# A second, narrower arm of the first product for jobs with at most 64 rows

## The chip, the cores and the metric

The kernel runs on one core of one Trainium2 chip. The metric is the device time of one execution in microseconds; several executions are timed and the median is taken.

## The reference

The kernel computes a recurrent attention and hands its output, token by token, to a mixture of experts in which every token goes to one expert. Cut to what matters here:

```python
B, H, S, D = 4, 8, 768, 48
x = attention(r, k, v, w, u)                # (B*S, H*D): 3072 tokens x 384
logits = x @ w_gate + modality_bias[modality_id]        # 8 experts
e_idx = argmax(logits)
gate_w = softmax(logits)[e_idx]
for e in range(8):
    mask = e_idx == e
    h = maximum(x[mask] @ w1[e], 0)         # 384 -> 1024
    out[mask] = gate_w[mask] * (h @ w2[e])  # 1024 -> 384
```

With the drawn inputs three of the eight experts get tokens: 1569, 1354 and 149.

## The kernel before, in words

The first part of the kernel works through the attention in 24 units of 128 tokens. As tokens are finished they are written as rows to a place of their expert, sorted by expert. While the later units run, nine fixed "slots" already compute 9 x 128 rows of the most popular expert. Of its 1569 rows 417 are left for later.

What is left is done in jobs. A job is up to 128 rows of one expert: 4 jobs for the 417 rows (the last holds 33), 11 for the 1354 (the last holds 74) and 2 for the 149 (the last holds 21), in this order, 17 in all. A job that has fewer rows still computes 128; what stands in the other rows is written nowhere. The first job (key "a") stands ahead of the loop; `tc.For_i` (L1434) runs the other 16, one in each turn, with the same instructions. Its bound `nj` comes from the device.

Which rows and which expert a job has is told by a table that `jobs` (L764 and following) works out on VectorE while the last slots run. It has one column per job (40 at most) and three rows: the first row's number (ROW), a code that says what has to be done for a change of expert (CODE), and the expert to load next (MORE). The table is computed with one job per partition, in `field`. L863 spreads it (product with the identity, `jd`), one matmul of TensorE (L866, `ptab`) brings it onto one partition, and VectorE casts it to integers (`tab`, L868). `at` (L873) reads one entry into a register of the engines that need it: SyncE reads ROW and MORE, ScalarE and VectorE read CODE.

Every number of the matmuls' inputs is split into a high and a low 16-bit half. A job's first product (`up`, `raise_`, L997) multiplies the transposed rows `mxT` by the first weights: `whi` against the high and the low rows, `wlo` against the high rows, three pieces of depth 128 each, so nine terms for each of eight blocks of 128 hidden values: 72 pairs of a weight load and a matmul with 128 columns, one column per row of the job. It goes in three groups of 4, 2 and 2 blocks, each into one tile `phb`. ScalarE takes the high half of the relu out of it (L1001, `hh`), VectorE the low half (L1006, `hl`). The second product (`term`, L1067) has 24 terms of 384 columns: eight of `whi` and eight of `wlo` with `hh` (`high_terms`), and eight of `whi` with `hl` (`low_terms`).

The turn of the loop is staggered by one: it begins with the low terms of the job before, whose output is then scaled, given to GpSimd and written (`put`). Then come the first product of the turn's own job, the load of the next weights (`next_load`, when the table asks), the copy of the following job's rows into place (`take_in`, L1402), and the high terms. The rows of the next job are fetched ahead by SyncE at the turn's start (`turn`). Where the expert changes (turns 4 and 15), ScalarE and VectorE split the new weights: `first_half` at the end of the turn before, `change` with 3, 4 and 5 in the turn itself. These stand under `tc.If`, which ScalarE and VectorE test with the code (L1413, L1424); TensorE tests nothing in a turn but the loop's own end. The order in each engine's queue is that in which the code is written (`manual_schedule`).

Of the kernel before, what the change touches and what calls it, by code (L numbers as in the profile page):

```python
# [12 lines left out]
I32 = mybir.dt.int32  # L13
I16 = mybir.dt.int16
AF = mybir.ActivationFunctionType
ALU = mybir.AluOpType
AX = mybir.AxisListType

P = 128
# [6 lines left out]
E = 8  # L26
# [13 lines left out]
NJ = 40  # L40
# [14 lines left out]
MS = ('DVE', 'Activation', 'PE', 'SP', 'Pool')  # L55
ROW, CODE, MORE = range(3)
SP, ACT, AD = (mybir.EngineType.SP,), (mybir.EngineType.Activation,), (mybir.EngineType.Activation, mybir.EngineType.DVE)
WQ = 2 * WC // NQ
# [6 lines left out]
class _Kernel:  # L65
# [213 lines left out]
    def setup3(self):  # L279

        c, v = self.c, self.nc.gpsimd
        gi, li = c.tile([P, STEPS], I32, name="gridi"), c.tile([P, 1], I32, name="linei")
        self.grid, self.linep, self.least = c.tile([P, STEPS], F32, name="grid"), c.tile([P, 1], F32, name="linep"), c.tile([P, E], F32, name="least")
        self.bits, self.line1 = c.tile([P, STEPS], F32, name="bits"), c.tile([P, 1], F32, name="line1")
        zeros = lambda name, shape: c.tile(shape, F32, name=name)
        self.jb, self.cum, self.ol = zeros("jb", [P, E + 2]), zeros("cum", [P, E + 1]), zeros("ol", [P, 5, E + 1])
        v.iota(gi, pattern=[[-1, STEPS]], base=STEPS - GONE, channel_multiplier=1)
        for q in range(STEPS):
            v.memset(self.bits[:, q : q + 1], float(1 << q))
        v.tensor_scalar_add(self.line1, self.line, -1.0)  # L290
        v.iota(li, pattern=[[0, 1]], base=0, channel_multiplier=P)
        for t in (self.jb, self.cum, self.ol, self.least):
            v.memset(t, 0.0)
        self.two = zeros("two", [P, 2, E])
        self.nc.scalar.copy(self.two[:, 0], self.idx)
        v.memset(self.least[:, :2], 1.0)
        v.tensor_copy(self.grid, gi)
        v.tensor_copy(self.linep, li)
# [473 lines left out]
    def jobs(self):  # L772


        nc, c = self.nc, self.c
        v = nc.vector
        new = lambda name, shape=[P, E], dt=F32: c.tile(shape, dt, name=name)
# [47 lines left out]
        v.scalar_tensor_tensor(ol[:, 2, 1:], act[:, 1:], float(-GONE), cum[:, 1:], ALU.mult, ALU.add)  # L825
        v.tensor_copy(ol[:, 3, 1:], cs)
        yield
        od, jr = new("od", [P, 5, E]), new("jr", [P, 5])
        v.tensor_sub(od, ol[:, :, 1:], ol[:, :, :E])
        yield  # L830
        v.scalar_tensor_tensor(od, cs.unsqueeze(1).to_broadcast([P, 5, E]), self.line, od, ALU.is_le, ALU.mult)
        yield
        v.reduce_sum(jr, od, axis=AX.X)
        yield
        field, past = new("field", [P, 3]), new("past", [P, 1])
        v.tensor_scalar(past, jr[:, 1:2], self.line, float(E * CAP), ALU.is_le, ALU.mult)
# [18 lines left out]
        v.reduce_sum(b, due, axis=AX.X)  # L855
        v.tensor_mul(field[:, MORE : MORE + 1], jr[:, 4:5], now)
        yield
        v.scalar_tensor_tensor(field[:, CODE : CODE + 1], now, float(1 << STEPS), b, ALU.mult, ALU.add)
        yield

        wide = [NJ, 3, NJ]
        d = new("jd", [P, 3, NJ])
        v.tensor_mul(d[:NJ], field[:NJ].unsqueeze(2).to_broadcast(wide), self.id32[:NJ, :NJ].unsqueeze(1).to_broadcast(wide))  # L863
        yield "pe"
        pt = self.ps_s.tile([P, 512], F32, tag="s", name="ptab")
        nc.tensor.matmul(pt[:1, : 3 * NJ], self.ones[:NJ, 0:1], d[:NJ].rearrange("p k j -> p (k j)"), start=True, stop=True)  # L866
        self.tab = new("tab", [1, 3, NJ], I32)
        v.tensor_copy(self.tab.rearrange("p k j -> p (k j)"), pt[:1, : 3 * NJ])  # L868
        yield
# [119 lines left out]

    def raise_(self, ph, f0, fb, t=0):  # L990

        hi, lo = self.whi, self.wlo
        terms = [(hi, dc, xq) for dc in range(DC) for xq in (dc, DC + dc)] + [(lo, dc, dc) for dc in range(DC)]
        for i, (w, dc, xq) in enumerate(terms):
            for q in range(fb):
                c0 = (f0 + q) * DM + dc * P
                self.nc.tensor.matmul(ph[:, q * P : (q + 1) * P], w[:, c0 : c0 + P], self.xT[:, xq, t * P : (t + 1) * P], start=i == q == 0, stop=i == len(terms) - 1, skip_group_check=True)  # L997

# [8 lines left out]

    def up(self, key, beside=lambda: None, late=False):
        later = []
        sizes = [4, 2, 2]  # L1010
        for g, fb in enumerate(sizes):
            f0 = sum(sizes[:g])
            ph = self.ps_a.tile([P, 512], F32, tag="big", name=f"ph{key}{g}")
            self.raise_(ph, f0, fb)
            self.relu_high(ph, f0, fb)
# [74 lines left out]
    def run(self):  # L1090
# [343 lines left out]
        with tc.For_i(1, nj, 1, iteration_sync="reg_based") as i, tc.manual_schedule(engines={getattr(mybir.EngineType, e) for e in MS[:4]}):  # L1434
            self.turn(0, self.at(ROW, i, E * CAP, SP, 1), mn, xn)
            code = self.at(CODE, i, 2 << STEPS, AD)
            self.low_terms(po)
            square(code)
# [4 lines left out]
            beside = iter([lambda: change(code, 5), lambda: self.scales("2")])  # L1443
            self.up("b", lambda: next(beside, lambda: None)(), True)
            next_load()
# [48 lines left out]
```

## Time and profile before

| | us |
|---|---|
| median of 3 runs | 353.31 |
| lowest, highest | 352.26, 354.82 |
| profiled execution, its own time | 353.3 |
| span of the profiled execution | 351.5 |
| TensorE busy in the span | 330.6 |

The span goes from the first to the last instruction; the execution's own time has 1.8 us more around it. PE is TensorE's matmuls, PEld its weight loads, PEldq its sequencer (registers, branches, semaphore steps), DVE VectorE, ACT ScalarE, POOL GpSimd, SP SyncE. Durations overlap: a matmul is shown from its start to its last result (219 ns at 128 columns), and the next starts before that.

### The profile page before, as it was taken

The numbers are of one execution on the slowest core, as the hardware profiler recorded it, in microseconds if no ns is written. First come the engines' busy times: TensorE is split into PE (matmuls) and PEld (weight loads), VectorE is DVE, ScalarE is ACT, GpSimd is POOL, SyncE is SP. The second block draws the span as 40 slices with busy tenths as digits, with TensorE's granted clock in tenths as the row PEclk, the third lists the DMA queues.
The fourth block names the chain that finished last, engine by engine and source line by source line (L and its number), as shares of the span: only waits on it lengthen the run. The fifth ranks groups of instructions, "written<-read, shape, count | busy, mean of one in ns | idle before, by whom it ended". The sixth has DMA issues, their size and how long they took to land. (4 is left out here: it accounts for less than half of the span.)

```text
span 351.5 us, 15420 instructions
## 1 busy us (share of the span) xinstructions
PE 330.6 (94%) x5555; PEld 269.6 (77%) x5555; DVE 220.0 (63%) x740; ACT 179.5 (51%) x476; POOL 154.6 (44%) x230
## 2 busy tenths in 40 slices
PE   7999998969899997999999999998999999999993
PEld 3888898868768885978888777776778888777771
DVE  6878898799898956498458843348423332334850
ACT  7678776867957644667542222247222224553820
POOL 8888678776646762435265711112111120121221
PEclk9999999878999998999999999999999999999999
DMA  6767677999539998736334632116722111112110
GB/s 194 214 157 166 141 174 214 319 263 211 138 112 195 265 208 235 173 103 122 92 92 137 229 118 64 45 45 207 224 53 59 45 45 45 45 45 67 35 45 5
DMA packets 56798, 46.96 MB, mean 134 GB/s; under 512 B 42920, under 2 KB 50359, under 8 KB 56496
## 3 DMA queue, kind: packets, MB, share of 16 engines
q1 hardware_dynamic: 53552, 36.86, 44.2%
q0 software_dynamic: 3200, 9.47, 7.7%
q8 instruction: 31, 0.51, 0.7%
q14 instruction: 15, 0.12, 0.1%
HBM read 26.03 MB, written 11.83 MB: 108 GB/s over the span
## 5 line engine op out<-in xcount | busy, mean ns | idle before, releaser
L997 PEld LDWEIGHTS <-whi 128*128 128x128 f16 x1248 | 72.4, 98 | 3.6 <-issue 0.9
L1067 PEld LDWEIGHTS <-hh 128*128 128x128 f16 x416 | 38.7, 98 | 29.5 <-ACT hh L1001 3.1
L997 PE MATMUL phb<-mxT,whi 128*128 128x128 f16 x768 | 50.7, 219 | 0.0
L410 ACT ACTIVATE dv<-kv,d 128x48 f32<-128x48 f32 x172 | 43.1, 324 | 2.3 <-POOL gap L664 1.8
L1001 ACT ACTIVATE hh<-phb 128x256 f16<-128x256 f32 (+1 forms) x48 | 21.4, 453 | 32.6 <-PE L997 16.9
L997 PEld LDWEIGHTS <-wlo 128*128 128x128 f16 x624 | 37.7, 98 | 0.0
L371 POOL TENSOR_TENSOR rk<-rc,kc 112x512 f32<-112x512 f32 x20 | 25.7, 1286 | 25.0 <-DVE ebx L309 12.0
L430 DVE TENSOR_TENSOR at<-psc,mask 128x512 f32<-128x512 f32 x48 | 31.7, 682 | 6.0 <-PE psc L424 6.0
L1006 DVE SCALAR_TENSOR_TENSOR hl<-phb,hh 128x256 f16<-128x256 f32 (+1 forms) x48 | 24.1, 511 | 17.5 <-ACTq L1424 15.0
L1087 DVE TENSOR_SCALAR fac<-mt,wf 128x1 f32<-128x1 f32 x17 | 3.6, 213 | 49.1 <-ACTq L1424 36.1
L359 POOL TENSOR_TENSOR rc<-ud,powr 112x512 f32<-112x512 f32 (+1 forms) x25 | 31.1, 1248 | 3.6 <-DMA ud<-in_pd 2.6
L966 POOL TENSOR_TENSOR seenb<-otb,putb 128x1 int32<-128x1 int32 x16 | 3.0, 188 | 65.1 <-ACTq L1424 53.2
L1067 PEld LDWEIGHTS <-hl 128*128 128x128 f16 x208 | 19.8, 99 | 14.7 <-issue 2.4
L424 PE MATMUL psc<-rc,kc 64*64 64x128 f32 (+1 forms) x768 | 29.7, 294 | 1.4 <-POOL rc L359 0.7
L957 ACT ACTIVATE otb<-po,fac 128x384 f32<-128x384 f32 x16 | 9.2, 578 | 41.8 <-PE phb L997 41.8
L665 POOL DMA_INDIRECT rows<-row,posi x24 | 24.9, 1039 | 10.4 <-DVE pr L742 3.3
L1067 PE MATMUL po<-whi,hh 128*128 128x384 f16 x136 | 28.3, 327 | 1.1 <-ACT hh L1001 1.0
L997 PE MATMUL phb<-mxT,wlo 128*128 128x128 f16 x384 | 29.3, 219 | 0.0
L1067 PE MATMUL po<-wlo,hh 128*128 128x384 f16 x136 | 28.0, 326 | 1.3 <-DVE wlo L943 1.3
L424 PEld LDWEIGHTS psc<-rc,kc 64*64 64x64 f32 (+1 forms) x768 | 22.9, 143 | 7.9 <-issue 2.7
L943 DVE SCALAR_TENSOR_TENSOR wlo<-raw,ws,whi 128x1024 f16<-128x1024 f32 (+1 forms) x20 | 27.0, 1389 | 1.2 <-ACT whi L938 1.2
L997 PE MATMUL phs<-mxT,whi 128*128 128x128 f16 x432 | 27.2, 219 | 0.0
(272 smaller groups left out, 663.4 us busy)
## 6 DMA issues: line engine op xcount, KB each, us to landing
kv<-in_pt SPq DMA_DIRECT2D x21, 384.0 KB, 5.5
raw<-in_w SPq DMA_DIRECT2D x12, 512.0 KB, 4.7
ud<-in_pd SPq DMA_DIRECT2D x12, 384.0 KB, 6.0
raw<-in_w SPq DMA_DIRECT2D x2, 1536.0 KB, 6.4
ud<-in_pd SPq DMA_DIRECT2D x12, 192.0 KB, 2.7
rows<-pad SPq DMA_DIRECT2D x10, 193.0 KB, 3.1
kv<-in_pt SPq DMA_DIRECT2D x6, 192.0 KB, 3.7
rows<-row,posi POOLq DMA_INDIRECT x24, 4.5
```

What stands on the lines that cost most here:

```text
L359: nc.gpsimd.tensor_mul(u["rc"][:TOP, s], u["rT"][:TOP, s], self.powr[:TOP, s])
L371: nc.gpsimd.tensor_mul(u["rk"][:TOP], u["rc"][:TOP], u["kc"][:TOP])
L410: nc.scalar.activation(u["dv"][:, sl], u["v"][:, sl], AF.Copy, scale=u["d"][:, h : h + 1])
L424: nc.tensor.matmul(u["ps"][j][s, pr * P : (pr + 1) * P], u["kc"][r, pr, s], u["rc"][r, pr, :], start=True, stop=True)
L430: nc.vector.tensor_mul(u["at"][:, j * NPR : (j + 1) * NPR, :], u["ps"][j].rearrange("p (q t) -> p q t", q=NPR), self.mask.unsqueeze(1).to_ ...
L665: i = nc.gpsimd.indirect_dma_start(out=self.rows, out_offset=bass.IndirectOffsetOnAxis(ap=u["posi"][:, b : b + 1], axis=0), in_=u["row"][: ...
L943: self.nc.vector.scalar_tensor_tensor(self.wlo[:, sl], self.raw[:, sl], sc, self.whi[:, sl], ALU.mult, ALU.subtract)
L957: self.nc.scalar.activation(ot, po[:, :DM], AF.Copy, scale=gf[:, t : t + 1])
L997: self.nc.tensor.matmul(ph[:, q * P : (q + 1) * P], w[:, c0 : c0 + P], self.xT[:, xq, t * P : (t + 1) * P], start=i == q == 0, stop=i == l ...
L1001: self.nc.scalar.activation(self.hh[:, f0 : f0 + fb, t * P : (t + 1) * P], p3, AF.Relu)
L1006: self.nc.vector.scalar_tensor_tensor(self.hl[:, f0 : f0 + fb, r], p3, 0.0, self.hh[:, f0 : f0 + fb, r], ALU.max, ALU.subtract)
L1067: self.nc.tensor.matmul(po[:, :DM], h[:, f, t * P : (t + 1) * P], w[:, c0 : c0 + DM], start=first, stop=last)
```

## The change

The table gets a fourth row HALF, which is 1 where a job has at most 64 rows left (`ROW + 64 >=` the end of the expert's rows, for which `ol` gets a sixth row). TensorE reads it into a register at the head of each turn. Around each of the three groups of the first product stands a branch with two arms: the short arm runs the first term of each group over 128 columns and the other eight over 64, the other arm is as before. The relu and the second product stay as they are, and job "a" ahead of the loop takes no branch.

```diff
-ROW, CODE, MORE = range(3)
+ROW, CODE, MORE, HALF = range(4)
+FIELDS = 4
@@ jobs
+        v.tensor_add(ol[:, 5, 1:], first_row, n)
         yield
-        od, jr = new("od", [P, 5, E]), new("jr", [P, 5])
+        od, jr = new("od", [P, 6, E]), new("jr", [P, 6])
...
         v.tensor_mul(field[:, MORE : MORE + 1], jr[:, 4:5], now)
+        v.scalar_tensor_tensor(field[:, HALF : HALF + 1], field[:, ROW : ROW + 1], float(P // 2), jr[:, 5:6], ALU.add, ALU.is_ge)
...
-        wide = [NJ, 3, NJ]
-        d = new("jd", [P, 3, NJ])
+        wide = [NJ, FIELDS, NJ]
+        d = new("jd", [P, FIELDS, NJ])
@@ raise_
-    def raise_(self, ph, f0, fb, t=0):
+    def raise_(self, ph, f0, fb, t=0, half=None):
+
+        if half is not None:
+            with self.tc.If(half > 0) as short:
+                self.raise_all(ph, f0, fb, t, P // 2)
+            with short.Else():
+                self.raise_all(ph, f0, fb, t)
+        else:
+            self.raise_all(ph, f0, fb, t)
+
+    def raise_all(self, ph, f0, fb, t, n=P):
...
         for i, (w, dc, xq) in enumerate(terms):
+            m = n if i else P
             for q in range(fb):
                 c0 = (f0 + q) * DM + dc * P
-                self.nc.tensor.matmul(ph[:, q * P : (q + 1) * P], w[:, c0 : c0 + P], self.xT[:, xq, t * P : (t + 1) * P], start=i == q == 0, stop=i == len(terms) - 1, skip_group_check=True)
+                self.nc.tensor.matmul(ph[:, q * P : q * P + m], w[:, c0 : c0 + P], self.xT[:, xq, t * P : t * P + m], start=i == q == 0, stop=i == len(terms) - 1, skip_group_check=True)
@@ the loop
             code = self.at(CODE, i, 2 << STEPS, AD)
+            half = self.at(HALF, i, 1, PE)
...
-            self.up("b", lambda: next(beside, lambda: None)(), True)
+            self.up("b", lambda: next(beside, lambda: None)(), True, half)
```

TensorE's queue at the head of the loop, before (`hl` is the low half of the relu, a name with `_own` is a semaphore that the loop keeps for each turn):

```order
L1434 COMPARE_AND_BRANCH [waits PE_I-4849_own]
L1434 UNCONDITIONAL_BRANCH
L1490 BRANCH_PREFETCH_HINT
L1067 LDWEIGHTS hl [waits DVE_I-4849_own,Activation_I-4849_own,DVE_49]
L1067 MATMUL po<-whi,hl 128x384
```

And the same place in the changed kernel:

```order
L1448 COMPARE_AND_BRANCH [waits PE_I-4851_own,PE_sequencer_I-4851_own]
L1448 UNCONDITIONAL_BRANCH
L1505 BRANCH_PREFETCH_HINT
L1081 LDWEIGHTS hl [waits DVE_I-4851_own,Activation_I-4851_own,DVE_49]
L876 ISA
L876 TENSOR_LOAD tab [waits DVE_49]
L1081 MATMUL po<-whi,hl 128x384
```

The table's load (L876) has come between the first weight load and the first matmul of the low terms. Further on TensorE goes from the last low term into the first group of the first product. Before:

```order
L1067 LDWEIGHTS hl
L1067 MATMUL po<-whi,hl 128x384
L997 ISA
L997 LDWEIGHTS whi [waits DVE_I-4849_own,Activation_I-4849_own]
L997 MATMUL phb_4924<-mxT,whi 128x128 [waits DVE_49]
```

And in the changed kernel, where the short arm comes first in the queue and the other arm (again from L1011 ISA on, with matmuls of 128x128) stands behind it:

```order
L1081 LDWEIGHTS hl
L1081 MATMUL po<-whi,hl 128x384
L996 COMPARE_AND_BRANCH
L1011 ISA
L1011 LDWEIGHTS whi [waits DVE_I-4851_own,Activation_I-4851_own]
L1011 MATMUL phb_4929<-mxT,whi 128x128 [waits DVE_49]
...
L1011 LDWEIGHTS wlo
L1011 MATMUL phb_4929<-mxT,wlo 128x64
L996 UNCONDITIONAL_BRANCH
L1011 ISA
L1011 LDWEIGHTS whi [waits DVE_I-4851_own,Activation_I-4851_own]
L1011 MATMUL phb_4929<-mxT,whi 128x128 [waits DVE_49]
```

A branch has come ahead of the group, and a jump from the end of the short arm over the other; the same stands at the other two groups. From the loop's head to the next instruction behind the loop TensorE's queue has 164 rows more than before.

VectorE's queue where the table is made, before:

```order
L855 TENSOR_REDUCE jbit<-dues 128x1 [waits DVE_49]
L856 TENSOR_TENSOR field<-jr,now 128x1
L858 SCALAR_TENSOR_TENSOR field<-now,jbit 128x1 [waits DVE_49]
...
L863 TENSOR_TENSOR jd<-field,id_148 40x120 [waits DVE_49]
L868 CAST tab<-ptab 1x120 [waits PE_49]
```

In the changed kernel:

```order
L857 TENSOR_REDUCE jbit<-dues 128x1 [waits DVE_49]
L858 TENSOR_TENSOR field<-jr,now 128x1
L859 SCALAR_TENSOR_TENSOR field<-field,jr 128x1
L861 SCALAR_TENSOR_TENSOR field<-now,jbit 128x1 [waits DVE_49]
...
L866 TENSOR_TENSOR jd<-field,id_148 40x160 [waits DVE_49]
L871 CAST tab<-ptab 1x160 [waits PE_49]
```

One instruction (L859) has come ahead of the spread table `jd`, and `jd` and `tab` have 160 columns in place of 120.

## Rows read from the trace of the kernel before

**Rows 1.** The page: busy time by engine, and the first product's matmuls in the loop.
```profile
PE 330.6 (94%) x5555; PEld 269.6 (77%) x5555; DVE 220.0 (63%) x740; ACT 179.5 (51%) x476; POOL 154.6 (44%) x230
...
L997 PE MATMUL phb<-mxT,whi 128*128 128x128 f16 x768 | 50.7, 219 | 0.0
```

**Rows 2.** Waits of TensorE, 211 to 346 us: total us, times, longest.
```profile
PE po L1067 <- DVE wlo L943: 1.3, 2, 0.6
PE po L1067 <- ACT hh L1001: 1.0, 2, 0.5
PE po L1067 <- PEq L1490: 0.8, 1, 0.8
```

**Rows 3.** Windows: a full turn, a turn with a change of expert (columns named).
```profile
core 0: us, PE busy (x) PEld busy (x) DVE busy (x) ACT busy (x) POOL busy (x), PEclk, DMA share, GB/s
255.73:263.67 7.94, 7.94 (x98) 6.40 (x97) 2.63 (x11) 1.94 (x4) 1.36 (x3) 1.00 0.20 47
238.14:247.78 9.64, 8.45 (x98) 6.29 (x97) 8.13 (x17) 5.29 (x8) 1.98 (x3) 1.00 0.68 201
```

**Rows 4.** Timeline of TensorE in a full turn: start us, us.
```profile
255.73 1.50 PE L997 MATMUL phb<-mxT,whi 128*128 128x128 f16 x24
257.07 0.83 PE L997 MATMUL phb<-mxT,wlo 128*128 128x128 f16 x12
...
259.77 1.14 PE L1067 MATMUL po<-whi,hh 128*128 128x384 f16 x6
...
262.37 1.46 PE L1067 MATMUL po<-whi,hl 128*128 128x384 f16 x8
263.67 0.33 PE L997 MATMUL phb<-mxT,whi 128*128 128x128 f16 x3
```

**Rows 5.** Timeline of TensorE, 183.3 to 183.8 us, during the attention.
```profile
183.41 0.45 PE L568 MATMUL pr<-wghl,xT 128*128 128x16 f16 x12
183.72 0.27 PE L997 MATMUL phs<-mxT,whi 128*128 128x128 f16 x2
```

**Rows 6.** Groups of weight loads by form: the loads of the product in rows 5.
```profile
L568 PEld LDWEIGHTS <-xT 128*128 128x128 f16 x144 | 4.4, 96 | 0.8 <-issue 0.7
```

**Rows 7.** Line 1434, the loop's branch on TensorE's sequencer: ns min/median/max, first and last.
```profile
L1434 PEldq COMPARE_BRANCH  x17: 88/221/238, 211.3 to 342.6; - x17
```

**Rows 8.** Line 873, table loads of ScalarE and VectorE in the loop.
```profile
L873 ACTq TENSOR_LOAD <-tab x16: 273/279/325, 211.4 to 334.0; - x16
L873 DVEq TENSOR_LOAD <-tab x16: 311/316/332, 214.0 to 337.6; - x16
```

**Rows 9.** Line 1395, TensorE's load of the number of jobs.
```profile
L1395 PEldq TENSOR_LOAD <-ctl x1: 485/485/485, 204.4 to 204.4; - x1
```

**Rows 10.** Line 997, 262 to 264.5 us: TensorE's sequencer ahead of its weight loads.
```profile
L997 PEld LDWEIGHTS <-whi x16: 97/98/98, 263.5 to 264.5; 128*128 128x128 f16 x16
...
L997 PEldq FUSED_REGOPS  x1: 42/42/42, 262.2 to 262.2; - x1
```

**Rows 11.** Line 1067 in the first turn (210.5 to 213.5 us), and TensorE's timeline there.
```profile
L1067 PEldq EVENT_SEMAPHORE  x2: 51/51/51, 212.9 to 213.2; - x2
...
213.00 1.46 PE L1067 MATMUL po<-whi,hl 128*128 128x384 f16 x8
```

**Rows 12.** VectorE's timeline where the table is made, and the wait before line 866.
```profile
203.06 0.15 DVE L856 TENSOR_TENSOR field<-jr,now 128x1 f32<-128x1 f32 x1
203.18 0.16 DVE L858 SCALAR_TENSOR_TENSOR field<-now,jbit 128x1 f32<-128x1 f32 x1
...
204.04 0.27 DVE L863 TENSOR_TENSOR jd<-field,id 40x120 f32<-40x120 f32 x1
...
  DVE jd L863: 0.3, 1
```

**Rows 13.** DMA queues: instructions on the page; every queue from 211 to 343 us.
```profile
q8 instruction: 31, 0.51, 0.7%
...
q1 hardware_dynamic: 16110, 6.45, 20.7%
q0 software_dynamic: 1024, 2.92, 5.9%
```

More of the change, by code (lines that the diff above doesn't have):

```diff
@@ L55 @@
 MS = ('DVE', 'Activation', 'PE', 'SP', 'Pool')
-ROW, CODE, MORE = range(3)
-SP, ACT, AD = (mybir.EngineType.SP,), (mybir.EngineType.Activation,), (mybir.EngineType.Activation, mybir.EngineType.DVE)
+ROW, CODE, MORE, HALF = range(4)
+FIELDS = 4
+SP, ACT, PE, AD = (mybir.EngineType.SP,), (mybir.EngineType.Activation,), (mybir.EngineType.PE,), (mybir.EngineType.Activation, mybir.EngineType.DVE)
 WQ = 2 * WC // NQ
@@ L285, in setup3 @@
         zeros = lambda name, shape: c.tile(shape, F32, name=name)
-        self.jb, self.cum, self.ol = zeros("jb", [P, E + 2]), zeros("cum", [P, E + 1]), zeros("ol", [P, 5, E + 1])
+        self.jb, self.cum, self.ol = zeros("jb", [P, E + 2]), zeros("cum", [P, E + 1]), zeros("ol", [P, 6, E + 1])
         v.iota(gi, pattern=[[-1, STEPS]], base=STEPS - GONE, channel_multiplier=1)
@@ L826, in jobs @@
         v.tensor_copy(ol[:, 3, 1:], cs)
+        v.tensor_add(ol[:, 5, 1:], first_row, n)
         yield
-        od, jr = new("od", [P, 5, E]), new("jr", [P, 5])
+        od, jr = new("od", [P, 6, E]), new("jr", [P, 6])
         v.tensor_sub(od, ol[:, :, 1:], ol[:, :, :E])
         yield
-        v.scalar_tensor_tensor(od, cs.unsqueeze(1).to_broadcast([P, 5, E]), self.line, od, ALU.is_le, ALU.mult)
+        v.scalar_tensor_tensor(od, cs.unsqueeze(1).to_broadcast([P, 6, E]), self.line, od, ALU.is_le, ALU.mult)
         yield
@@ L834, in jobs @@
         yield
-        field, past = new("field", [P, 3]), new("past", [P, 1])
+        field, past = new("field", [P, FIELDS]), new("past", [P, 1])
         v.tensor_scalar(past, jr[:, 1:2], self.line, float(E * CAP), ALU.is_le, ALU.mult)
@@ L865, in jobs @@
         pt = self.ps_s.tile([P, 512], F32, tag="s", name="ptab")
-        nc.tensor.matmul(pt[:1, : 3 * NJ], self.ones[:NJ, 0:1], d[:NJ].rearrange("p k j -> p (k j)"), start=True, stop=True)
-        self.tab = new("tab", [1, 3, NJ], I32)
-        v.tensor_copy(self.tab.rearrange("p k j -> p (k j)"), pt[:1, : 3 * NJ])
+        nc.tensor.matmul(pt[:1, : FIELDS * NJ], self.ones[:NJ, 0:1], d[:NJ].rearrange("p k j -> p (k j)"), start=True, stop=True)
+        self.tab = new("tab", [1, FIELDS, NJ], I32)
+        v.tensor_copy(self.tab.rearrange("p k j -> p (k j)"), pt[:1, : FIELDS * NJ])
         yield
@@ L1006, in relu_low, with up @@
         self.nc.vector.scalar_tensor_tensor(self.hl[:, f0 : f0 + fb, r], p3, 0.0, self.hh[:, f0 : f0 + fb, r], ALU.max, ALU.subtract)
-    def up(self, key, beside=lambda: None, late=False):
+    def up(self, key, beside=lambda: None, late=False, half=None):
         later = []
@@ L1013, in up @@
             ph = self.ps_a.tile([P, 512], F32, tag="big", name=f"ph{key}{g}")
-            self.raise_(ph, f0, fb)
+            self.raise_(ph, f0, fb, half=half)
             self.relu_high(ph, f0, fb)
```

## Prediction

> **What bounds the kernel now.** I read the busy times first: TensorE is busy 94% of the span and no other engine over 63% [rows 1]. Then the place of the change, the loop over jobs: the waits of TensorE there come to 3.1 us, in five places, out of 135 us, and 0.8 of it lies behind the loop's end [rows 2]. [...] So an ordinary turn is as long as its TensorE instructions, and whatever is taken from them comes off the time at once. A turn in which the expert changes lasts 9.64 us with TensorE busy 8.45: there VectorE's weight splits (busy 8.13) set part of the length [rows 3].
>
> The changed part is the first product. In a full turn it starts at 255.73 and the second product at 259.77 [rows 4]: 4.04 us for 72 pairs of weight load and matmul, one pair each 55.8 ns (24 of them from 255.73 to 257.07 gives the same). The rest of the turn is 24 terms of the second product at 162 ns (262.37 to 263.67 for the last eight), and nothing in them changes.
>
> **How many jobs take the short arm.** The first product's matmuls of the loop, 768 on the high weights at 48 a job [rows 1], say 16 turns. The drawn tokens give 17 jobs, the first ahead of the loop. Only the last job of an expert can hold at most 64 rows: 417 left rows of the most popular expert end with 33, 1354 end with 74, which is too many, 149 end with 21. The job ahead of the loop and turns 1 to 3 are the first expert's, so turns 3 and 16 are short; 14 of 16 run the full arm, and pay whatever the branch costs for nothing.
>
> **The short arm.** Of 72 matmuls 8 stay 128 columns wide and 64 become 64 wide. If the columns set the pace, a pair falls from 55.8 to 28 ns: 64 x 27.8 = 1.8 us a job. Can weights be loaded at that pace? 12 matmuls of another product, each with its own 128 x 128 load of some 96 ns, pass in 0.31 us (183.41 to 183.72), 26 ns a pair, and these are 16 wide at most [rows 5, 6]. So the load does not bind at 28, and 1.8 us is the upper end. The lower end comes from TensorE's sequencer: it must stay ahead at twice the pace. In the full arm it does its register steps and semaphore steps while TensorE works off pairs already queued; in the short arm group 0 alone has five such steps among its pairs, and each of the three groups ends with a jump over the full arm. A taken branch of TensorE's sequencer takes 221 ns [rows 7] and its next instruction comes some 0.1 us later, and three jumps and the compares may eat 1 us and more; with the register steps on top 0.2 us is left as the lower end. I take 0.75 us a job, nearer the lower end, because the rows with 26 ns show a run of only 12 pairs without any step between. Two jobs: -1.5 us (ends -0.4 and -3.6).
>
> [...]
>
> **The load and the branches in the full turns.** TensorE's sequencer reads the new field at the loop's head. It never did so in the loop before. ScalarE and VectorE do: one table load is 279 and 316 ns there [rows 8], with its address steps 0.5 to 0.6 us; TensorE's own one load ahead of the loop took 485 ns [rows 9]. Then a compare-branch ahead of each group, taken in a full turn, about 0.3 us. Together ahead of group 0: 0.8 us, up to 1.1. The cover: the sequencer takes group 0's first step at 262.2, and TensorE loads that group's first weights at 263.5 [rows 10]. That lead of 1.3 us is work already queued (the second product's low terms), so the added 0.8 to 1.1 is hidden, with 0.2 to 0.5 to spare. Behind the load on its engine stand the low terms, for which no other engine waits within the lead. The branches of groups 1 and 2 cost 0.3 us each against the pairs queued by then; no wait of TensorE for its sequencer inside the loop stands in the rows [rows 2], and I cost them at nothing. If that cover is gone, a full turn pays up to 0.3 us ahead of group 0 and up to 0.3 us at each of the later groups. Below nothing is excluded: the full arm issues what it issued before. I take 0 for 14 turns; ends 0 and 8 us.
>
> The first turn has no such lead: its sequencer passes a semaphore step at 212.9, and the first low term starts at 213.00 [rows 11]. The load stands between that term's weights and its matmul, so its 0.5 us is exposed once, and with the branch behind it some 0.1 more: +0.6 us (ends 0.2 and 1.0).
>
> **The table.** Two VectorE instructions more, each about 0.15 us like their neighbours, one of them and the wider product of field and identity (0.27 us at 120 columns) in front of TensorE's table matmul, which already waits 0.3 us for that product [rows 12]. The first addition and the wider differences lie beside the attention units' end, off the path. A wider product and one more small instruction: +0.25 us, and the wider matmul and cast a bit: +0.3 us (ends 0 and 0.6).
>
> **The sum**, against the profiled execution's 353.3 us (span 351.5 and 1.8 us around it), which is the median of the runs as well: -1.5 + 0 + 0.6 + 0.3 = -0.6, so 352.7 us. With all the ends of the short arm, the first turn and the table at once it is 349.9 (-3.4) to 354.5 (+1.2); they are not all met together, so the likeliest case's own range is 350.8 to 354.2.
>
> **Rivals.**
> First: the loop's code no longer fits what the sequencer keeps. TensorE's part of the loop grows from some 220 to some 385 instructions, because both arms of the three groups stand in it. The profile's instruction queue moved 31 pieces of 16 KB, and through the whole loop before not one came [rows 13]. 5555 matmuls with their loads [rows 1], less 15 repeated turns of 97 pairs [rows 3], are 8200 instructions, so a piece holds about 260. A loop of 220 touches two pieces; one of 385 touches two or three, and by where the program stands, three. If the sequencer keeps only two, every turn fetches the third and then the first again. A piece takes about 1.3 us on the queue (0.7% of 16 x 351.5 us, over 31). The point from which it decides is what the added load and branch leave of the lead, 0.2 to 0.5 us: a fetch at the loop's head or at a jump that keeps the sequencer longer shows on TensorE. A fetch of 1.3 us less 0.5 would show 0.8 us a turn, two fetches 2.1 us; but ahead of the loop the pieces came while earlier code ran, so part of one lies beside work. I price 0.5 us a turn: over 16 turns +8 on the forecast, 360.7 us; at 0.8 it is 365.5, and two bare fetches a turn would be +34. For it: the growth, and that the arm skipped by a full turn sends the sequencer past code in jumps. Against: the trace never shows a piece evicted, so it doesn't say how many are kept. Chance 0.32.
> [...]
>
> Second: the sequencer is late in the full turns without any fetch: the load takes 485 ns each time, or the branches of groups 1 and 2 show. 0.3 us in 14 turns: +4.2, so 356.9 us. For it: the lead left over is only 0.2 to 0.5 us. Against: the sequencer is ahead everywhere in the loop. Chance 0.08.
>
> Third: the full column gain, 1.8 us twice, with the load and the table hidden: -3.6, so 349.7 us. For it: 26 ns a pair in the trace. Against: the register steps and jumps. Chance 0.05. That the change doesn't do what it says (a short arm at the old pace, as where the weight load sets 55.8 ns): 353.3 + 0.6 + 0.3 = 354.2 us; chance 0.07, against it [rows 5, 6].
>
> **Chances.** The forecast has 0.48. 1% is 3.5 us, about what a measurement of this kernel can tell from no change. The second and the third rival lie at that bound (+3.6 and -3.6), and half of each counts to either side. Within 1%: 0.48 + 0.07 + 0.04 + 0.02 = 0.61. Slower by over 1%: 0.32 + 0.04 = 0.36. Faster by over 1%: 0.03. The range runs from 350.8, which leaves out the third rival, to 363.0, which takes in the first up to 0.6 us a turn, somewhat over half of its chance: some 0.19 is left out.
>
> **What would show it.** Right: full turns of 7.9 us with no wait for TensorE's sequencer, two turns of about 7.2 us, no instruction pieces after the loop's start, one gap of half a microsecond in the first turn. Wrong: pieces of TensorE's code in every turn, with a wait of TensorE at the loop's head or at a group's start (first rival); full turns of 8.2 us or more without such pieces (second); short turns of 6.1 us (third) or of 7.9 (fourth).

## The result, and the profile after

The changed kernel takes 357.34 us (median of 6 runs, 356.81 to 358.09); the kernel before, run beside it, 352.98 us (6 runs). The ratio is 1.0122, with a 95% interval of 1.0086 to 1.0158: 3.0 to 5.6 us slower. The forecast was 352.7 us and no change that can be measured. 357.34 lies inside the given range (350.8 to 363.0), near the second rival's 356.9, but the kernel became slower where it was to stay the same.

The page of the changed kernel, the lines that answer to [rows 1] and [rows 13]:

```profile
span 355.1 us, 15527 instructions
...
PE 329.5 (93%) x5555; PEld 263.8 (74%) x5556; DVE 221.8 (62%) x742; ACT 179.4 (51%) x476; POOL 154.7 (44%) x230
...
q8 instruction: 33, 0.54, 0.7%
...
L1011 PE MATMUL phb<-mxT,whi 128*128 128x128 f16 (+1 forms) x768 | 49.2, 216 | 0.0
```

TensorE has as many matmuls as before and is busy 1.1 us less; two pieces of code more were fetched in the whole execution. The waits of TensorE from 209 to 348 us, to be held against [rows 2]:

```profile
PE po L1081 <- ACT hh L1015: 2.2, 6, 0.5
PE po L1081 <- issue: 2.0, 10, 0.2
PE po L1081 <- DVE wlo L946: 1.3, 2, 0.6
PE phb L1011 <- issue: 1.1, 2, 0.5
PE po L1081 <- DVE hl L1020: 0.6, 2, 0.3
PE po L1081 <- DVE mt L1416: 0.6, 1, 0.6
```

New is "issue", a wait for nothing that the profile shows: ten times before the second product (the repeats of before, below, have one of 0.3 to 0.4 us) and twice before the first. Where this is, TensorE's timeline of an ordinary turn shows (the bracket is the idle time before the row):

```profile
261.33 0.49 PE L1081 MATMUL po<-wlo,hh 128*128 128x384 f16 x2
262.02 0.32 PE L1081 MATMUL po<-whi,hl 128*128 128x384 f16 x1 [0.20 <-issue]
```

The two high terms start at 261.33 and 261.49, and a term takes 162 ns, so the low terms of the next turn could start at 261.65; they start at 262.02, 0.37 us late. The sequencer's rows on the loop's line 1448 and on line 876, the table load, in the same place:

```profile
L1448 PEldq COMPARE_BRANCH  x1: 227/227/227, 260.9 to 260.9; - x1
...
L876 PEldq FUSED_REGOPS  x1: 46/46/46, 261.6 to 261.6; - x1
L876 PEldq TENSOR_LOAD <-tab x1: 296/296/296, 261.7 to 261.7; - x1
```

The sequencer reaches the loop's branch at 260.9, only 0.7 us before TensorE is free, and the load (261.6 to 262.0) stands between it and the first low term. In the first profile of before it was there 1.4 us ahead: branch at 261.0, low terms at 262.37 ([rows 4]).

```profile
L1434 PEldq COMPARE_BRANCH  x1: 221/221/221, 261.0 to 261.0; - x1
```

What a turn costs is seen in windows of the changed kernel: the whole loop, an ordinary turn, the short turn 3, the turn with the change of expert behind it (columns as in [rows 3]).

```profile
209.54:348.51 138.97, 130.62 (x1553) 98.13 (x1552) 56.53 (x192) 50.26 (x90) 23.50 (x47) 1.00 0.25 67
253.66:262.02 8.36, 8.16 (x97) 6.29 (x97) 2.66 (x11) 1.95 (x4) 1.36 (x3) 1.00 0.20 47
226.50:234.90 8.40, 7.31 (x97) 5.00 (x97) 3.10 (x12) 3.20 (x7) 1.36 (x3) 1.00 0.19 47
234.90:245.29 10.39, 8.66 (x97) 6.27 (x97) 9.18 (x18) 6.87 (x10) 1.83 (x3) 1.00 0.66 192
```

In the short turn TensorE is busy 0.85 us less than in the ordinary one (7.31 to 8.16), and the turn is no shorter (8.40 to 8.36). So two things are to be explained: what an ordinary turn lost, and why the short arm won nothing.

### The profile page after: what moved, and what is told of

Read it like the earlier page. It is cut to its first block, busy times and chain, and to the rows that moved or that the text cites. A ratio compares the mean times of both kernels' runs of the same rounds, so it can differ in the third digit from the quotient of the medians.

```text
span 355.1 us, 15527 instructions
## 1 busy us (share of the span) xinstructions
PE 329.5 (93%) x5555; PEld 263.8 (74%) x5556; DVE 221.8 (62%) x742; ACT 179.4 (51%) x476; POOL 154.7 (44%) x230
## 5 line engine op out<-in xcount | busy, mean ns | idle before, releaser
L1011 PEld LDWEIGHTS <-whi 128*128 128x128 f16 x1248 | 70.5, 98 | 4.5 <-issue 2.3
L1081 PEld LDWEIGHTS <-hh 128*128 128x128 f16 x416 | 37.6, 98 | 34.3 <-ACT hh L1015 7.7
L1011 PE MATMUL phb<-mxT,whi 128*128 128x128 f16 (+1 forms) x768 | 49.2, 216 | 0.0
L1011 PEld LDWEIGHTS <-wlo 128*128 128x128 f16 x624 | 37.1, 98 | 1.3 <-issue 1.2
L1081 PE MATMUL po<-whi,hh 128*128 128x384 f16 x136 | 29.2, 328 | 2.5 <-ACT hh L1015 2.2
L1011 PE MATMUL phb<-mxT,wlo 128*128 128x128 f16 (+1 forms) x384 | 28.7, 216 | 1.1 <-issue 1.1
L1081 PE MATMUL po<-whi,hl 128*128 128x384 f16 x136 | 24.8, 325 | 4.1 <-issue 2.0
L425 PE MATMUL psc<-rc,kc 64*64 64x128 f32 (+1 forms) x768 | 28.2, 282 | 0.4
L462 PE MATMUL py<-kv,at 128*64 128x48 f32 x768 | 27.3, 225 | 0.0
```

What stands on the lines that cost most here:

```text
L425: nc.tensor.matmul(u["ps"][j][s, pr * P : (pr + 1) * P], u["kc"][r, pr, s], u["rc"][r, pr, :], start=True, stop=True)
L462: nc.tensor.matmul(py[t, sl], u["at"][:, j * NPR + pr, t], u["v"][:, sl], start=c == h == 0, stop=h == H - 1, skip_group_check=True)
L1011: self.nc.tensor.matmul(ph[:, q * P : q * P + m], w[:, c0 : c0 + P], self.xT[:, xq, t * P : t * P + m], start=i == q == 0, stop=i == len(t ...
L1081: self.nc.tensor.matmul(po[:, :DM], h[:, f, t * P : (t + 1) * P], w[:, c0 : c0 + DM], start=first, stop=last)
```

## Experiments

Loop times below run from the first low term of the first turn to the first low term behind the loop, in the one profiled execution of each run. Between repeats of one kernel they agree within 0.1 us, but for the first profile of before (below), while the whole execution varies by over 1%. Medians are given beside. A time "in the turn" counts from the turn's first low term. The runs stand by subject: on record, e1 to e4 came first, then b1 and b2, then e10, e12, x1 and x2, then y1 to y3, and b3 and a3 last. Each theory's letter is explained in the first expectation that uses it.

### Both kernels again

No edit: the kernel before three times more (b1, b2, b3), and the changed kernel once more (a3).

> The kernel before, unchanged, profiled again. Theory K (the relu of group 1 starts late, 5.6 us into the turn instead of 4.9, because of something in the changed kernels): it starts at 4.90 again in every ordinary turn, the loop takes 131.9 us. Theory S (late or not late is a state of the execution that the kernel before has as well): it may start at 5.6, turns of 8.0 us, loop 133 to 136 us.

> The same once more: theory K 4.90 us and a loop of 131.9 us; theory S either value.

> The kernel before, unchanged, with a profile from the same chip as the next run. If TensorE's signals stand still during GpSimd's write here: relu of group 1 at 5.6 us of an ordinary turn, lead 0.7 us, loop near 135.7 us. If not (as in the very first profile): 4.9 us, 1.3 us, loop near 131.9 us.

> The changed kernel on the same chip. Theory G: where before shows the relu at 5.6 us, this one has turns of 8.35 us and a loop some 3 us longer than before's. Where before shows it at 4.9 us, this one has turns of 7.95 us and a loop within 1 us of before's (as x2 against x1, 132.1 to 131.6 us). Rival (the change costs 3 us whatever before's state): 3 us more in both.

Windows of the third repeat of before: the loop, an ordinary turn, turn 3, a change of expert; then the loop of the repeat of the changed kernel, from the same chip.

```profile
210.24:345.91 135.67, 130.36 (x1555) 100.95 (x1552) 56.56 (x192) 50.22 (x90) 23.36 (x47) 1.00 0.25 68
252.64:260.74 8.10, 8.10 (x99) 6.31 (x97) 2.64 (x11) 1.94 (x4) 1.36 (x3) 1.00 0.19 49
226.26:234.35 8.09, 8.09 (x98) 6.31 (x97) 2.72 (x12) 2.82 (x6) 1.36 (x3) 1.00 0.21 49
234.35:244.65 10.30, 8.54 (x100) 6.29 (x97) 9.08 (x16) 7.25 (x10) 1.79 (x2) 1.00 0.57 177
```

```profile
208.83:347.88 139.05, 130.73 (x1555) 98.20 (x1553) 56.55 (x192) 50.28 (x90) 23.59 (x47) 1.00 0.25 66
```

The first profile of before is the odd one. Its loop takes 131.86 us (213.00 to 344.86); the three repeats take 135.68, 135.66 and 135.67, on two chips. The changed kernel takes 138.97 and 139.05. So before and after stand 3.3 to 3.4 us apart in the loop, which lies within the interval of the whole time (3.0 to 5.6 us); the median difference of 4.4 us leaves 1 us outside the loop that nothing here accounts for. The repeats' whole times are 353.32 and 354.63 us (b1 and b2, one execution each), 353.78 us (b3, median of 9) and 358.9 us (a3, median of 3), the last two with 352.85 us for before beside them: ratios 1.0039 (0.9992 to 1.0086) and 1.0115 (1.0002 to 1.0228). The part ahead of the loop was longer in the first profile (213.0 us, against 209.3, 210.4 and 210.2), so that its total gave nothing away.

The difference between the two kinds of turn is in ScalarE's timeline. First the ordinary turn of the first profile, which starts at 254.43, then the one of the repeat, which starts at 252.64:

```profile
258.25 0.60 ACT L1001 ACTIVATE hh<-phb 128x512 f16<-128x512 f32 x1 [1.50 <-PE L997]
259.32 0.38 ACT L1001 ACTIVATE hh<-phb 128x256 f16<-128x256 f32 x1 [0.48 <-PE phb L997]
260.46 0.38 ACT L1001 ACTIVATE hh<-phb 128x256 f16<-128x256 f32 x1 [0.76 <-PE po L1067]
```

```profile
256.46 0.60 ACT L1001 ACTIVATE hh<-phb 128x512 f16<-128x512 f32 x1 [1.50 <-PE phb L997]
258.34 0.38 ACT L1001 ACTIVATE hh<-phb 128x256 f16<-128x256 f32 x1 [1.28 <-PE po L1067]
259.48 0.38 ACT L1001 ACTIVATE hh<-phb 128x256 f16<-128x256 f32 x1 [0.76 <-PE po L1067]
```

From the turn's start the relus come at 3.82, 4.89 and 6.03 us in the first, at 3.82, 5.70 and 6.84 in the second: that of group 1 waits 0.8 us longer, though TensorE has written group 1 at the same 4.5 us in both. The sequencer of TensorE waits for that relu ahead of the fifth high term, so it reaches the loop's branch 0.8 us later, 0.7 us ahead of TensorE (260.74) in place of 1.4:

```profile
L1434 PEldq COMPARE_BRANCH  x1: 216/216/216, 260.0 to 260.0; - x1
```

Theory S holds: the delay is in before as well, in all three repeats. It was wrong to take the first profile for the kernel.

The packed traces also hold the time of every step of TensorE's semaphore, the signal that an instruction is finished (one for each weight load and matmul, 194 in a turn), which the views above don't print. In the turn of the first profile the steps come 30 ns apart without a break from 1.47 to 6.06 us. In the turn of the repeat they come 30 ns apart too, but between 3.16 and 4.53 us there are only two: two silences of 0.60 and 0.74 us (some 15 steps of the turn are missing from the record there). Then they go on at 30 ns. The step for the end of group 1 comes at 4.65 us in the first and at 5.46 in the second, 0.24 us ahead of the relu in both. So ScalarE is not slower; it is told later.

### The parts of the change one by one

The table row alone (e1; meant as the row and the load; in the trace of this run TensorE has no table load, only a semaphore step, as nothing used the register):

```diff
-            self.up("b", lambda: next(beside, lambda: None)(), True, half)
+            self.up("b", lambda: next(beside, lambda: None)(), True)
```

> The table row and TensorE's register load at the loop's head stay, the branches and the short arm go. Theory A (the load and the mid-stream branches each use up part of the sequencer's lead, and only together exceed it): the sequencer reaches the head at 6.6 us of the turn as before, the load brings the low terms to 7.7, full turns stay at 7.94 us; first turn +0.3 to 0.5; total 353.0 to 354.0 us. Rival B (the load by itself is the cost): full turns 8.3 us, total 358 to 359.

Loop 135.38 us, median 352.55 us (before 353.39), ratio 0.9965, 0.9921 to 1.0008. It tells only that the wider table costs the loop nothing; on the load it says nothing, and neither theory is helped.

The branches alone (e2):

```diff
         take_in()
+        half = self.at(HALF, slice(1, 2), 1, PE)
         po = self.ps_y.tile([P, 512], F32, tag="y", name="po")
...
-            half = self.at(HALF, i, 1, PE)
```

> TensorE loads HALF once ahead of the loop (value 0), so every turn runs the full arm through all three branches and no turn has a table load of TensorE. Theory A: the relus of groups 1 and 2 still start 0.7 us later than before, the sequencer reaches the loop's head at 7.2 to 7.3 us instead of 6.6, but the low terms are just in time: turns 7.95 to 8.05 us, total 353 to 355. Rival C (the branches by themselves are the cost): turns 8.3 us and total 358 or more.

Loop 135.35 us, turns 8.02 us, median 354.47 us (before 353.39), ratio 1.0034, 0.9994 to 1.0074. Three taken branches a turn and the doubled code cost nothing, as theory A had it; rival C falls. The times of the relus are those of the repeats of before (5.62 and 6.76 us): the branches did not make them late.

The load behind the low terms, with the branches (e3):

```diff
-            half = self.at(HALF, i, 1, PE)
             self.low_terms(po)
...
             self.due(m2)
+            half = self.at(HALF, i, 1, PE)
```

> As the changed kernel, with TensorE's table load moved behind the low terms, ahead of group 0. Theory A: the low terms start without a gap and the load lies beside them; full turns 7.95 to 8.05 us, total 352.5 to 354.5. Rival B or C: where the load stands makes no difference, turns 8.3 to 8.4 us and total 357 to 358.

Loop 138.90 us, turns 8.4 us, median 357.91 us (before 353.39), ratio 1.013, 1.0037 to 1.0223. Theory A's number (8.0 us) fell: the low terms do start without a gap now, but the gap has moved one stage on, to the start of the first product, where TensorE's timeline has it:

```profile
255.29 1.46 PE L1081 MATMUL po<-whi,hl 128*128 128x384 f16 x8
256.95 1.57 PE L1011 MATMUL phb<-mxT,whi 128*128 128x128 f16 x24 [0.20 <-issue]
```

The eight low terms end at 256.59 by their pace, and the first product starts at 256.95. The load and the branch of group 0 stand in a row there, and the 0.7 us of lead doesn't hold both.

### The load with the free branch, and the load where the sequencer has time

A branch at group 2 only, the load at the head (e10):

```diff
-            self.raise_(ph, f0, fb, half=half)
+            self.raise_(ph, f0, fb, half=half if g == 2 else None)
```

> As the changed kernel with TensorE's table load at the loop's head, but a branch at group 2 only, where the sequencer has time (it waits there for the relu of group 1 anyway). Theory B2 (the load at the head is the cost by itself, because the sequencer comes there only 0.7 us before TensorE is free, and not 1.3): full turns 8.3 to 8.4 us, loop 138 to 139.5 us, total as the changed kernel, 356 to 358. Theory A (only load and all branches together exceed the lead): turns 8.05 us, loop 135.5, total 352.5 to 354.

The load behind group 0, branches at groups 1 and 2 (e12):

```diff
-            self.raise_(ph, f0, fb, half=half)
+            self.raise_(ph, f0, fb, half=half if g else None)
+            if half is not None and g == 0:
+                half = half()
...
-            half = self.at(HALF, i, 1, PE)
...
-            self.up("b", lambda: next(beside, lambda: None)(), True, half)
+            self.up("b", lambda: next(beside, lambda: None)(), True, lambda: self.at(HALF, i, 1, PE))
```

> TensorE's table load moved behind group 0, branches at groups 1 and 2 only (group 0 always in full). Theory B2: the sequencer is ahead there, so load and branches are hidden: turns 8.05 us, loop 135 to 136 us, total 352.5 to 354.5. Rival (a table load of TensorE in a turn costs wherever it stands): turns 8.3 us or more, loop 138 or more.

An ordinary turn of e10, then an ordinary one and short turn 3 of e12:

```profile
254.49:262.86 8.37, 8.21 (x98) 6.30 (x97) 2.64 (x11) 1.94 (x4) 1.36 (x3) 1.00 0.19 47
```

```profile
251.97:260.03 8.06, 8.06 (x100) 6.32 (x98) 2.64 (x11) 1.94 (x4) 1.36 (x3) 1.00 0.19 49
225.56:233.66 8.10, 7.73 (x100) 5.67 (x98) 2.72 (x12) 2.82 (x6) 1.36 (x3) 1.00 0.20 49
```

With the load at the head and one branch the loop takes 138.67 us (median 357.57, before 353.29; ratio 1.011, 1.0058 to 1.0163): nearly all of the change's cost. With the load behind group 0 it takes 135.78 us (median 353.83; ratio 1.0005, 0.9965 to 1.0045): nothing of it. Together with e2 (all three branches, no load in the turn, no cost) this leaves the place of one table load as the cost, and theory B2 holds against A. The short turn of e12 is no shorter than its ordinary one, with TensorE busy 0.33 us less.

### Why the short arm wins nothing

The kernel before with 64 columns in every job, no branch, no load (e4; the first product's terms behind the first are left out for rows 65 to 128 of all jobs of the loop):

```diff
-            self.raise_(ph, f0, fb)
+            self.raise_(ph, f0, fb, 0, P // 2 if key == "b" else P)
```

> The kernel before, with 64 columns in 64 of 72 matmuls of the first product in every turn, no branch and no load; it leaves out the first product's terms of rows 65 to 128 in every job of the loop. Theory D (ScalarE is told of a group's end no earlier than some 30 ns per TensorE instruction allow, so the relus start as late as in a full turn): the first product ends 1.9 us earlier, but the second waits for the relus; turns 7.0 to 7.4 us, total 341 to 346. Rival (the columns count in full): relus move forward with the matmuls, turns 6.1 us, total 322 to 326.

The turn that starts at 250.42, its window, TensorE and then ScalarE:

```profile
250.42:258.46 8.04, 7.02 (x99) 5.10 (x97) 2.64 (x11) 1.95 (x4) 1.36 (x3) 1.00 0.20 49
```

```profile
251.72 0.97 PE L998 MATMUL phb<-mxT,whi 128*128 128x128 f16 x24
...
254.18 0.25 PE L998 MATMUL phb<-mxT,wlo 128*128 128x64 f16 x2
254.96 0.37 PE L998 MATMUL phb<-mxT,wlo 128*128 128x64 f16 x4 [0.53 <-issue]
255.20 0.81 PE L1068 MATMUL po<-whi,hh 128*128 128x384 f16 x4
256.50 0.50 PE L1068 MATMUL po<-whi,hh 128*128 128x384 f16 x2 [0.49 <-ACT hh L1002]
```

```profile
254.24 0.60 ACT L1002 ACTIVATE hh<-phb 128x512 f16<-128x512 f32 x1 [1.50 <-PE phb L998]
256.06 0.38 ACT L1002 ACTIVATE hh<-phb 128x256 f16<-128x256 f32 x1 [1.23 <-PE po L1068]
257.20 0.38 ACT L1002 ACTIVATE hh<-phb 128x256 f16<-128x256 f32 x1 [0.76 <-PE po L1068]
```

The turn takes 8.04 us, with TensorE busy for 7.02 of it. The loop of 136.54 us holds one turn of 10.36 us, in which TensorE stood still for 1.87 us and then went on for a while at a lower granted clock (0.57 in the 3.4 us that followed), with terms of the second product 0.32 us apart, twice the usual 0.162; in b3 the same turn takes 8.81 us. The other fifteen turns are together 0.7 us shorter than in b3, none by more than 0.2. Median 354.13 us (before 353.39; ratio 0.9991, 0.9933 to 1.0048). So 14 short turns more win next to nothing. The matmuls themselves are as fast as the columns say: the 24 pairs on the high weights of group 0, four of them wide, take 0.81 us, so 20 narrow pairs take 0.58 us, 29 ns each. Group 0 is through 2.6 us into the turn, in place of 3.5. But its relu starts at 3.82 us (254.24 less 250.42), to the hundredth where it starts after 128 columns, and those of groups 1 and 2 at 5.64 and 6.78. The steps of TensorE's semaphore tell why: they come 30 ns apart here too, from 1.48 to 3.19 us, then with silences of 0.56 and 0.69 us up to 4.50, then 30 ns apart again, though TensorE passes a narrow pair, two steps, in 29 ns. The second product then waits for the relus (0.49 us before the fifth term). The rival that counted on the columns is out by 30 us. Theory D named the right limit, 30 ns for each instruction, but expected 7.0 to 7.4 us, by the relus of the first profile, which has no silences.

### The write of GpSimd

What holds the relu of group 1 up? In the repeat of before GpSimd makes its indirect write in the very time between group 0's end and that relu:

```profile
255.85 0.99 POOL L967 DMA_INDIRECT out<-otb,putb  x1 [0.55 <-issue]
```

That is 3.2 to 4.2 us into the turn, where the semaphore's steps fall silent. Both kernels were run without it (x1 before, x2 changed); the rows of the loop's jobs are then not written, and this work is left out:

```diff
+        if key == "b":
+            return
         i2 = nc.gpsimd.indirect_dma_start(
```

> The kernel before without GpSimd's indirect write of the rows of the loop's jobs (this work is left out). Theory G (while GpSimd writes that DMA's descriptors, the signals of TensorE's finished instructions stand still for 0.7 us, which makes the relu of group 1 late): the relu starts at 4.9 us of the turn, the sequencer is at the head 1.3 us ahead, turns 7.95 us. Rival (its lateness has nothing to do with GpSimd): 5.65 us, 0.7 us and 8.07 us as in the two further profiles of before.

> The changed kernel without that write (the same work left out). Theory G: the relu of group 1 starts near 4.9 us, the sequencer's lead is 1.3 us again, which covers load and branch: turns 7.95 to 8.0 us, loop 131 to 133 us. Rival: 8.35 us and 138 to 139 us as with the write.

ScalarE in the turn of before without the write that starts at 250.74, then the changed kernel without it: an ordinary turn, short turn 3, the change of expert.

```profile
254.55 0.60 ACT L1003 ACTIVATE hh<-phb 128x512 f16<-128x512 f32 x1 [1.57 <-PE L999]
255.63 0.38 ACT L1003 ACTIVATE hh<-phb 128x256 f16<-128x256 f32 x1 [0.48 <-PE phb L999]
256.77 0.38 ACT L1003 ACTIVATE hh<-phb 128x256 f16<-128x256 f32 x1 [0.76 <-PE po L1069]
```

```profile
257.34:265.29 7.95, 7.95 (x100) 6.39 (x98) 2.63 (x11) 1.95 (x4) 0.38 (x2) 1.00 0.15 25
231.28:238.96 7.68, 7.12 (x99) 4.97 (x97) 3.09 (x12) 3.20 (x7) 0.38 (x2) 1.00 0.14 26
238.96:249.36 10.40, 8.66 (x98) 6.27 (x97) 9.18 (x18) 6.87 (x10) 0.38 (x2) 1.00 0.63 187
```

Without the write the relus come at 3.81, 4.89 and 6.03 us, the loop of before takes 131.63 us and that of the changed kernel 132.11 (the profiled execution of x2 is 6.4 us longer than its median, but the loop only starts 6.1 us later in it): the 3.3 us between the two are 0.5. Theory G holds in what it says of the delay; of the descriptors that it names the traces show nothing, only one `DMA_INDIRECT` of GpSimd of 0.99 us in a turn. In the eleven traces that have the write in its place, not counting the first profile of before, the semaphore is silent for 1.0 to 1.4 us in all in each of turns 1 to 3, 5 to 10, 14 and 16; in x1 and x2 it never is. Ordinary turns pay nothing for the load and the branches, and the short turns are 0.27 (turn 3) and 0.53 us (turn 16) shorter than those of x1. What is left over sits in the two turns with a change of expert, 0.75 and 0.49 us longer than in x1 (10.40 against 9.64 us in the first). There the low terms start 0.49 us late, as the sequencer comes to the head only 0.6 us ahead without any write of GpSimd; the other 0.27 us in the first is a later start of the second product, which waits 0.30 us for the relu of group 0, so that what turn 3 had won is gone again. Medians 350.83 and 349.81 us (before 353.29; ratios 0.99, 0.9848 to 0.9953, and 0.9912, 0.9884 to 0.994): no difference between the two kernels that could be measured.

### Moving the write

The write held back until the relu of group 2 is done, by a GpSimd instruction that reads its result; in before (y1), in the changed kernel (y2), and in the one with the load behind group 0 (y3):

```diff
-            self.put(po, 0, "b")
+            write = self.give(self.take(po, 0, "b"), 0, "b", self.hh[:, FB - 1, 0:2].bitcast(I32))
+            next(write)
...
+            next(write)
             next_load()
```

> The kernel before with GpSimd's indirect write held back until the relu of group 2 is done (one small GpSimd instruction that reads its result). Theory G: the write's descriptors are made where no relu waits for TensorE, so the relu of group 1 starts at 4.9 us, the lead at the head is 1.3 us, turns 7.95 us, loop 131.5 to 132.5 us, total 348.5 to 350.5 us. Rival (the write costs wherever it stands, the delay only moves to the low terms or the next relu): turns 8.0 us or more, loop 134 to 136, total 352 to 354.

> The changed kernel with the same late write. Theory G: load and branches are covered again in ordinary turns (7.95 us), a short turn ends 0.6 us earlier of which part is lost at the next head (7.3 to 7.7), the turns with a change of expert are 0.5 to 0.7 us longer than in y1; loop 131.5 to 133 us, total 348.5 to 351, no longer slower than y1 by more than 1 us. Rival: 8.35 us a turn and 356 to 358.

> Table load behind group 0, branches at groups 1 and 2 only, and the late write. Theory G: no full turn pays, the change turns neither; a short turn gains 0.4 to 0.9 us; loop 130.5 to 132 us, total 348 to 350, the fastest of the three by up to 1.5 us. Rival: the short arm gains nothing here either, loop as y1 within 0.3 us.

Before with the late write: an ordinary turn, the turn behind a change of expert, the last turn.

```profile
251.68:259.62 7.94, 7.94 (x99) 6.39 (x97) 2.64 (x11) 1.95 (x4) 1.41 (x5) 1.00 0.22 50
240.93:251.68 10.75, 8.26 (x99) 6.31 (x97) 3.32 (x16) 1.92 (x4) 1.34 (x5) 1.00 0.56 169
333.28:346.27 12.99, 8.11 (x98) 6.33 (x97) 3.40 (x15) 1.95 (x4) 1.55 (x5) 0.90 0.15 39
```

The ordinary turns take 7.94 us in y1 and in y2 alike, and the semaphore is never silent in them, so the load costs nothing where the relus come as early as in the first profile. But this is no second proof of theory G. Before took 346.99 us on the chip of these three runs, 6 us less than on the others, and no profile of before from it was taken. The loop of y1 starts at 207.42 us; with the first profile's loop of 131.86 us, the 6.6 us behind it and the 1.8 us around the span, before would take an estimated 347.7 us, with the repeats' loop 351.5. So before probably ran there without the delay that the late write was to take away; the changed kernel with the write in its place was not run on that chip.

The total went the wrong way in all three. The last turn grows from 9.0 to 13.0 us, because TensorE's low terms behind the loop wait until GpSimd has drained its queue (4.88 us idle in y1): the drain takes 5.14 us, as in before, but begins behind the late write, 7.3 us into the turn in place of 3.2. The turn behind the first change of expert grows from 8.0 to 10.75 us in y1 (11.8 in y2 and y3): ScalarE's next scaled output waits for the late write before it (8.90 us idle), and TensorE's high terms wait for ScalarE. The loops take 138.85, 141.12 and 140.48 us, the medians are 356.22, 356.87 and 355.79 us (ratios 1.0209, 1.028 and 1.0226, with intervals from 1.0111 to 1.037). None of the three is a better kernel.

## Why the prediction was wrong, point by point

**What bounds the kernel.** That an ordinary turn is as long as its TensorE instructions, and that whatever is taken from them comes off the time at once, rests on [rows 2] and on the full turn of [rows 3], busy for 7.94 of 7.94 us. The first half is nearly right (8.10 of 8.10 in the repeat). The second is false: e4 takes 1 us of TensorE's work out of a turn, and the turn stays at 8.04 us. A chain lies right beside the busy engine: TensorE's finished instructions are signalled, ScalarE makes the relu, TensorE's fifth high term waits for it. The signals go out 30 ns apart and pause around GpSimd's write (for 1.0 to 1.4 us in all), so this chain is as long as the work, and no row of a busy engine shows it.

**The short arm.** Priced at -0.75 us a job, nearer the lower end of 0.2 to 1.8 because of the sequencer's steps. The pace was right (29 ns a pair) and the sequencer was not the limit; the relus were, and the gain is 0 (8.40 us against 8.36). Without GpSimd's write it is 0.27 and 0.53 us in the two short turns.

**The load and the branches in the full turns.** This is the step that failed: "That lead of 1.3 us is work already queued ..., so the added 0.8 to 1.1 is hidden". The size of the lead was wrong: it came from an execution whose relus came 0.8 us earlier than in the three repeats. There the sequencer is 0.7 us ahead at the loop's head, and 0.7 us at group 0 too (first step at 261.2, first weights at 261.9). From the loop's branch to the first low term the changed kernel's sequencer needs 1.1 us (260.9 to 262.02), so 0.3 to 0.4 us show. The place was wrong too: the lead was taken at group 0 [rows 10], but the load stands at the loop's head, one stage earlier, between the first low term's weights and its matmul (in the changed kernel it ends at 262.0, and that matmul starts at 262.02). That alone would have cost little, since the first profile's lead is 1.4 us at the head, and in x2 the load is hidden there. The branches at groups 1 and 2, costed at nothing, cost nothing (e2).

**The first turn.** 0.6 us was the forecast; the changed kernel's two profiles have 8.63 and 8.35 us there, against 7.95 in the repeat of before: 0.4 to 0.7. Right.

**The table.** 0.3 us ahead of the loop can't be told: the loop's start differs by over 1 us between executions of one kernel.

**The sum.** Against b3, in the loop: -1.5 for the two short turns should have been +0.3 and 0; 0 for the full turns should have been +2.3 (a3: +2.7) for the 13 behind the first; the first turn's +0.6 was +0.7 (a3: +0.4). Ordinary turns pay 0.2 to 0.4 us each, the two with a change of expert 0.1, and two turns in which the next job's weights are moved were even shorter (8.44 and 8.37 against 8.81 and 8.62 us). Both large terms erred to the same side, and nothing made up for it.

**The rivals.** The second (the sequencer late in full turns, 0.3 us in 14 turns, 356.9 us) is what happened, with the load as its cause (296 to 323 ns each, not 485), and it had been given a chance of 0.08. Against it stood that "the sequencer is ahead everywhere in the loop": it is, but by too little. The first (code that no longer fits) had 0.32, and it fell: the DMA queues of the changed kernel from 215 to 348 us are

```profile
q1 hardware_dynamic: 14448, 6.11, 19.5%
q0 software_dynamic: 961, 2.72, 5.6%
```

with no instruction queue among them, and e2, which has both arms, has before's turns (8.02 us, against 8.10 in b3). No run shows whether the changed loop reaches into a third piece, nor how many pieces the sequencer keeps; the two of the rival were an assumption. The fourth (no gain of the short arm) was true as an effect, though not by the weight load: a narrow pair passes in 29 ns.

## What to carry to other kernels

Before an operation is hung on a sequencer, find the places where that sequencer is least ahead of its engine, which here are the loop's head and the start of group 0, and put the operation where it is further ahead: the same table load cost 3 us of loop time at the head and nothing behind group 0. A row that says an engine is busy without a gap doesn't say that less work makes the turn shorter: take the work out in an experiment (narrow matmuls in every turn) before a branch is built to take it out in some. And profile a kernel more than once before a margin of half a microsecond is read from it.

## What the runs showed of the hardware that was not expected

The relus of groups 1 and 2 start 1.14 us apart in every ordinary turn above, whatever the matmuls' width: 38 TensorE instructions lie between (18 pairs of group 2 and one of another product), 30 ns each; in the undelayed turns those of groups 0 and 1 start 1.07 or 1.08 us apart, with 36 instructions between, 30 ns each as well. With 64 columns a pair passes in 29 ns, and the relu starts no earlier. The traces have the cause: from 1.47 to 6.06 us of the first profile's turn, and from 1.48 to 3.19 us of e4's, the steps of TensorE's semaphore are 30 ns apart, one for each weight load and matmul, so that 72 narrow pairs are announced no faster than wide ones. Wide pairs (55.8 ns for two steps) run a little ahead of their signals as well. That fewer steps would help was not tested by a kernel that has fewer of them, nor whether an execution that is not traced has the same pace.

While GpSimd makes an indirect write in this place (0.99 us), the steps of the eleven traces named above fall silent for 1.0 to 1.4 us in all, and the relu that waits for TensorE comes 0.7 to 0.8 us later than without it (5.70 us against 4.89). In e4 TensorE itself stands still for 0.5 us (4.0 to 4.5 us into the turn), until the steps go on. Why the first profile of before has the same write at the same time (257.63 to 258.62 by its timeline), no silence and no delay stays open. That the delay comes with the write is shown by taking the write away; what path the two share is not.
